# One weight transfer of a long stream, issued in three pieces of 48, 8 and 8 rows

## The chip, the cores and the metric

The kernel runs on one core of a Trainium2 chip. The metric is the device time of one execution in microseconds (us); lower is better. The core's compute engines are TensorE (PE in the profile; its weight loads are shown apart as PEld), VectorE (DVE), ScalarE (ACT) and GpSimd (POOL). SyncE (SP) and POOL issue the DMA transfers of this kernel, and 16 DMA engines carry them out.

## The reference

Linear attention with the feature map elu + 1, then a spectral mixing of its output along the sequence: a real Fourier transform, a complex matrix for each of the 64 lowest frequencies ("modes"), the inverse transform, and a channel product with a rectifier.

```python
def _attn_ref(q, k, v):                        # 8 x 8 heads x 576 x 64
    def phi(x):
        return np.where(x > 0, x, np.exp(x) - 1.0) + 1.0
    q_p, k_p = (phi(q), phi(k))
    kv = np.einsum('bhsd,bhse->bhde', k_p, v)
    z = np.sum(k_p, axis=2)
    num = np.einsum('bhsd,bhde->bhse', q_p, kv)
    den = np.einsum('bhsd,bhd->bhs', q_p, z)[..., None] + 1e-06
    return (num / den).astype(np.float32)

def _moe_ref(x, w_r, w_i, w_ch):               # w_r, w_i: 64 x 512 x 512, float32
    B, S, D = x.shape                          # 8, 576, 512
    n_modes = w_r.shape[0]
    X = np.fft.rfft(x, axis=1)
    Y = np.zeros_like(X)
    Xr, Xi = (np.real(X[:, :n_modes]), np.imag(X[:, :n_modes]))
    Yr = np.einsum('bmd,mde->bme', Xr, w_r) - np.einsum('bmd,mde->bme', Xi, w_i)
    Yi = np.einsum('bmd,mde->bme', Xr, w_i) + np.einsum('bmd,mde->bme', Xi, w_r)
    Y[:, :n_modes] = Yr + 1j * Yi
    y = np.fft.irfft(Y, n=S, axis=1)
    u = x + y
    return (u + np.maximum(u @ w_ch, 0.0)).astype(np.float32)
```

The two weight tensors `w_r` and `w_i` are read once each and are by far the largest inputs: 64 modes x 2 parts x 1 MB.

## The kernel before

**First part (lines 370 to 405).** For each of the eight batch elements q, k and v are loaded by POOL, which casts them to 16 bits on the way, the attention is formed, and its output is transformed to the 64 modes, kept as `xt_c` in SBUF. Between these loads POOL already issues the first weights.

**The weight stream.** The 64 modes are worked on as 32 pairs, `p` = 0 to 31. `mode_pair(p)` (line 462) multiplies the 16 activation slices of a pair with its weight tile `w{p}` in 16 products (line 432, PSUM tile `P`), brings the result to SBUF (`evacuate`, lines 447 and 449, DVE for even pairs and ACT for odd ones), picks the two modes out of it (line 455), and fills the time up with other work from a list (`work_slot`: folding early modes into the output, channel products and so on) and with products that only keep PE busy (`keep_warm`, line 419).

**The weight tile and its two transfers.** `w{p}` has 128 partitions. `w_load(p, half, ...)` (line 112) is called for half 0 (from `w_r`) and half 1 (from `w_i`) and issues one transfer each time, line 117. The source of one transfer is two modes, 2 x 512 x 512 float32, read as 64 rows of 16 x 512 consecutive numbers (32 KB). Row r of half h goes to partition 2r + h, as bfloat16 (16 KB): 1 MB is written for each transfer, which the DMA casts on the way.

**What sets the order.** All issues are pinned to program order (`pin`). The tiles of pairs 0 and 1 and of all pairs from 5 on share two buffers (`W_KEEP = 2`, pool `wpool`); pairs 2 to 4 have buffers of their own. `mode_pair(p)` begins with `w_get(p)`, so that the transfers of pair p are issued in the order of the code before its products; they wait on POOL until the products of the pair that had the buffer, p - 2, are done. So while pair p is in transfer or in use, pair p + 1 is in transfer. POOL issues nothing else in this part of the program. A transfer's landing is told by a semaphore, which each of the 16 DMA engines steps once when its part is done; POOL's transfers take eight semaphores in turn.

**The end.** The last pair (`w_load_last`, `last_pair`, line 487) comes in eight smaller transfers, so that its last products (`y_last`, line 513) follow each small landing. After them the last modes are transformed, and the outputs are summed (lines 760 and 800) and stored by SP (lines 816 and 822).

Of the kernel before, what the change touches and what calls it, by code (L numbers as in the profile page):

```python
# [43 lines left out]
def kernel(  # L44
# [10 lines left out]
    nc = tc.nc  # L55
# [7 lines left out]
    NDW = 4 * NDC  # L63
# [42 lines left out]
    pin = tc.keep_in_program_order  # L106
    PIECES = (slice(0, 2), slice(2, 4), slice(4, 6), slice(6, 7), slice(7, 8))
    HALVES = [slice(0, 64), slice(64, 128)]

    LAST = NM // 2 - 1  # L110

    def w_load(p: int, half: int, pool, tag: str, bufs: int):
        if half == 0:
            w_in[p] = pool.tile([128, NDW, D], BF16, tag=tag, bufs=bufs, name=f"w{p}")
        two = (moe_w_r, moe_w_i)[half][2 * p : 2 * p + 2]
        pin(
            nc.gpsimd.dma_start(  # L117
                out=w_in[p][half::2], in_=two.rearrange("g (r dc) e -> (g r) dc e", dc=NDW)
            )
        )  # L120

    def w_load_last(pool, tag: str, bufs: int):
        w_in[LAST] = pool.tile([128, NDW, D], BF16, tag=tag, bufs=bufs, name=f"w{LAST}")
        for g in range(2):
            for half in range(2):
                rows_in = (moe_w_r, moe_w_i)[half][NM - 2 + g].rearrange("(p dc) e -> p dc e", dc=NDL)
                for dcs in PIECES if (g, half) == (1, 1) else (slice(0, NDL),):
                    dst = w_in[LAST][half::2, g * NDL + dcs.start : g * NDL + dcs.stop]
                    pin(nc.gpsimd.dma_start(out=dst, in_=rows_in[:, dcs, :]))
# [16 lines left out]
    def w_next():  # L146
        p, half = pending.pop(0)
        pool, tag, bufs = (wpool, "w", W_KEEP) if p < n_keep else (wpre, "wp", W_PRE)
        w_load(p, half, pool, tag, bufs)
# [258 lines left out]
    def w_get(p: int):  # L408
        if p not in w_in and p == LAST:
            w_load_last(wpool, "w", W_KEEP)  # L410
        elif p not in w_in:
            for half in range(2):
                w_load(p, half, wpool, "w", W_KEEP)
        return w_in[p]
# [14 lines left out]
    def product(P, x, n: int, w, dc: int, n_dc: int):  # L429
        c = dc % NDC * 32  # L430
        pin(
            nc.tensor.matmul(  # L432
                P[c : c + n, :], x, w[:, dc, :],
                start=(dc < NDC), stop=(dc >= n_dc - NDC), tile_position=(0, c),
                skip_group_check=True,
            )
        )

    def set_diagonal(p: int):
        for h in range(2):  # L440
            src = xt_v[HALVES[h], :, :, :, p].rearrange("p c t b -> p c (t b)")
            pin(nc.vector.tensor_copy(out=xz[p % 2][HALVES[h], :, h, :], in_=src))  # L442
# [19 lines left out]
    def mode_pair(p: int):  # L462
# [5 lines left out]
        for dc in range(NDW):  # L468
            product(P, xz[p % 2][:, dc].rearrange("p h n -> p (h n)"), 32, w, dc, NDW)
        if p + 1 < LAST:  # L470
            set_diagonal(p + 1)
# [15 lines left out]
    def last_pair():  # L487
        xl = ystage.tile([128, NDL, 2 * B], BF16, name="xl")
        for h in range(2):
            src = xt_v[:, (2 * h + 1) * NDC : (2 * h + 2) * NDC, :, :, LAST]  # L490
            pin(
# [3 lines left out]
            )  # L495
        w = w_get(LAST)
        kk = NM - 2
# [91 lines left out]
    def x_of(t: int):  # L589
        if t < B * NJJ:  # L590
            return x_main[t // NJJ][:, t % NJJ, :]
        i = t - B * NJJ
        return x_tail[i // 2][:, i % 2, :]
# [352 lines left out]
    for h, eng in enumerate((nc.sync, nc.gpsimd)):  # L946
        eng.dma_start(
            out=YZ_all[64 * h : 64 * h + 64 : NF // NL].rearrange("r b z d -> r b (z d)"),
            in_=last.rearrange("p z d -> p (z d)"),
# [15 lines left out]
    def sums_of(n: int, i: int):  # L965
# [8 lines left out]
            out=x_of(0), in0=accs[0][:, 0], scalar=0.0, in1=x_of(0), op0=ALU.max, op1=ALU.add  # L974
# [50 lines left out]
```

## Time and profile before

| what | value |
|---|---|
| median of 3 runs | 421.13 us |
| lowest, highest | 421.12, 421.89 us |
| span of the profiled execution (first to last instruction) | 419.4 us |
| mean granted clock of TensorE | 0.830 |
| PE, DVE, ACT, POOL busy, share of the span | 76%, 55%, 37%, 14% |
| read from HBM, written | 163.93 MB, 9.44 MB |
| weight transfers of 1024 KB, real and imaginary | 31 and 31 |
| their median time from issue to landing | 13.2 and 17.5 us |
| one issue on POOL (line 117), median | 544 ns |

The page divides the span into 40 slices of about 10.5 us and gives for each the busy share of an engine in tenths. The share of the DMA is that of the core's 16 DMA engines together:

```profile
PE   0369998999617875676767686988798877998993
DMA  8999999999999999999999999999999999998698
```

The chain of waits goes back from the last instruction to what released it, and so on; a line of it has the start, the length and what it was, all in us from the start of the span. A transfer in it reaches from its issue to its landing, so that time in line behind other transfers counts in. In the lists of packets, "under 512 B" counts the small ones; a transfer's completion is a packet of 4 bytes on each DMA engine. The queue "q0 software_dynamic" carries POOL's transfers, "q1 hardware_dynamic" SP's, and the queues with "instruction" the program code of the engines. A queue's share is the time that its packets took, of 16 engines over the stretch that is looked at.

### The profile page before, as it was taken

The numbers are of one execution on the slowest core, as the hardware profiler recorded it, in microseconds if no ns is written. First come the engines' busy times: TensorE is split into PE (matmuls) and PEld (weight loads), VectorE is DVE, ScalarE is ACT, GpSimd is POOL, SyncE is SP. The second block draws the span as 40 slices with busy tenths as digits, with TensorE's granted clock in tenths as the row PEclk, the third lists the DMA queues.
The fourth block names the chain that finished last, engine by engine and source line by source line (L and its number), as shares of the span: only waits on it lengthen the run. The fifth ranks groups of instructions, "written<-read, shape, count | busy, mean of one in ns | idle before, by whom it ended". The sixth has DMA issues, their size and how long they took to land.

```text
span 419.4 us, 7466 instructions
## 1 busy us (share of the span) xinstructions
PE 317.2 (76%) x3143; PEld 164.4 (39%) x3143; DVE 231.3 (55%) x509; ACT 154.2 (37%) x253; POOL 57.4 (14%) x100
## 2 busy tenths in 40 slices
PE   0369998999617875676767686988798877998993
PEld 0257776877301332222222233433343332453421
DVE  4588899785314563463645353464456443522794
ACT  4677798854201011000000233334253432330783
POOL 4222224210011211111111111111111111130000
PEclk9999999579855658665655599899899997899998
DMA  8999999999999999999999999999999999998698
GB/s 217 211 212 216 210 222 203 228 206 223 217 223 208 218 220 209 220 217 212 220 214 213 223 213 214 223 210 216 220 209 219 217 214 219 216 209 166 235 391 328
DMA packets 17073, 93.17 MB, mean 222 GB/s; under 512 B 2112, under 2 KB 3024, under 8 KB 12880
## 3 DMA queue, kind: packets, MB, share of 16 engines
q0 software_dynamic: 12496, 81.48, 93.4%
q1 hardware_dynamic: 4544, 11.22, 7.2%
q8 instruction: 24, 0.39, 0.3%
q14 instruction: 9, 0.07, 0.0%
HBM read 163.93 MB, written 9.44 MB: 413 GB/s over the span
## 4 chain that ended last, share of the span: by engine, by line
DMA 64%; PE 23%; DVE 4%; POOL 3%; ACT 3%; issue 2%; DVEq 0%; ACTq 0%; POOLq 0%
DMA w<-in_moe_w_i_dram 53%; DMA pick_sb<-row_pick 8%; PE P L432 6%; DMA k<-in_k_dram 3%; PE acc L760 3%; PE kvp L257 3%; PE acc L800 2%; POOL w L117 2%; PE z L726 1%; DVE x L293 1%; ACT ke L208 1%; PE xf L355 1%; PE zl L419 1%; PE qTp L237 1%; PE num L163 1%
## 5 line engine op out<-in xcount | busy, mean ns | idle before, releaser
L432 PE MATMUL P<-w,xz 128*32 128x512 bf16 x496 | 42.6, 475 | 37.6 <-DMA w<-in_moe_w_i_dram 35.4
L419 PE MATMUL zl<-wch,id 128*128 128x512 f16 x185 | 58.2, 466 | 0.0
L449 ACT CAST ys<-P 128x512 f16<-128x512 f32 x15 | 8.8, 586 | 132.4 <-PE P L432 132.4
L117 POOL DMA_DIRECT2D w<-in_moe_w_r_dram x31 | 17.3, 559 | 246.4 <-PE P L432 211.8
L447 DVE CAST ys<-P 128x512 f16<-128x512 f32 x17 | 11.8, 692 | 51.0 <-PE P L432 51.0
L706 PE MATMUL eps<-wch,xTw 128*128 128x512 f16 x144 | 39.3, 399 | 0.0
L432 PEld LDWEIGHTS <-xz 128*32 128x32 bf16 x496 | 12.6, 108 | 63.3 <-DMA w<-in_moe_w_i_dram 40.3
L163 PEld LDWEIGHTS <-qT 64*128 64x128 f16 (+1 forms) x640 | 22.6, 122 | 29.6 <-issue 15.6
L689 ACT CAST x16w<-x_main 128x512 f16<-128x512 f32 x32 | 19.8, 618 | 37.8 <-DVE x_main L687 37.8
L687 DVE TENSOR_TENSOR x_main<-ya,x_main 128x512 f32<-128x512 f32 x32 | 22.0, 689 | 16.5 <-PE ya L683 16.3
L257 PE MATMUL kvp<-vpad,ke 32*128 32x130 f16 x576 | 24.3, 263 | 8.9 <-ACT qT L244 6.1
L442 DVE COPY xz<-xt_c 64x256 bf16<-64x256 bf16 x62 | 23.0, 371 | 10.9 <-PE P L432 10.0
L419 PEld LDWEIGHTS <-id 128*128 128x128 f16 x185 | 18.9, 112 | 25.6 <-issue 14.3
L714 ACT CAST E<-eps 128x512 f16<-128x512 f32 (+1 forms) x40 | 21.2, 540 | 17.7 <-PE eps L706 17.7
L257 PEld LDWEIGHTS <-ke 32*128 32x128 f16 x576 | 22.3, 116 | 10.6 <-issue 8.6
L163 PE MATMUL nw<-kv_sb,qT 64*128 64x65 f16 (+1 forms) x320 | 18.2, 231 | 9.8 <-DVE x_tail L650 4.7
L237 PE MATMUL qTp<-id,qe 128*128 128x128 f16 x144 | 15.1, 289 | 10.6 <-DVE qe L221 9.5
L293 DVE TENSOR_TENSOR x<-num,rd 128x512 f16<-128x512 f32 x32 | 22.1, 692 | 1.1
L650 DVE TENSOR_TENSOR x_main<-nw,rd 128x256 f32<-128x256 f32 x32 | 11.2, 416 | 18.8 <-PE nw L163 18.8
L455 PE MATMUL yt<-pick_sb,ys 128*128 128x32 f16 (+1 forms) x128 | 8.8, 185 | 16.7 <-DMA pick_sb<-row_pick 9.4
L698 DVE COPY xTw<-xTp 128x512 f16<-128x512 f16 x36 | 15.0, 416 | 10.3 <-PE xTp L696 10.3
L208 ACT ACTIVATE qe<-q 128x1152 f16<-128x1152 f16 (+1 forms) x16 | 17.9, 1157 | 7.2 <-DMA q<-in_q_dram 7.1
(118 smaller groups left out, 507.5 us busy)
## 6 DMA issues: line engine op xcount, KB each, us to landing
w<-in_moe_w_r_dram POOLq DMA_DIRECT2D x31, 1024.0 KB, 13.2
w<-in_moe_w_i_dram POOLq DMA_DIRECT2D x31, 1024.0 KB, 17.5
out_dram<-x_main SPq DMA_DIRECT2D x12, 512.0 KB, 3.6
k<-in_k_dram POOLq DMA_DIRECT2D x8, 576.0 KB, 12.9
v<-in_v_dram POOLq DMA_DIRECT2D x8, 576.0 KB, 14.3
q<-in_q_dram POOLq DMA_DIRECT2D x7, 576.0 KB, 12.6
out_dram<-x_main SPq DMA_DIRECT2D x8, 256.0 KB, 4.0
q<-in_q_dram SPq DMA_DIRECT2D x2, 576.0 KB, 4.5
```

Of the source, the lines that this page charges most:

```text
L117: nc.gpsimd.dma_start(out=w_in[p][half::2], in_=two.rearrange("g (r dc) e -> (g r) dc e", dc=NDW))
L163: mm = nc.tensor.matmul(num[hpo][orow, c0 : c0 + 65], qT[rows, hpp, h2, cols], kv_sb[rows, hpp, h2, :])
L208: pin(nc.scalar.activation(out=ev[:, c], in_=heads(nm, b, c), func=AF.Exp))
L257: nc.tensor.matmul(kv_ps[:, h2, 0:130], phi["k", b][r0 : r0 + 32, j // NJ, j % NJ].rearrange("p o d -> p (o d)"), vp[r0 : r0 + 32, :, j, 0 ...
L293: nc.vector.tensor_tensor(out=dst.rearrange("p (o c d) -> p o c d", o=2, c=4), in0=nv[:, :, :, 0:64], in1=rden.unsqueeze(3).broadcast_to([ ...
L419: pin(nc.tensor.matmul(last_ps[0], id16, wch16[:, 0, :]))
L432: nc.tensor.matmul(P[c : c + n, :], x, w[:, dc, :], start=(dc < NDC), stop=(dc >= n_dc - NDC), tile_position=(0, c), skip_group_check=True,)
L442: pin(nc.vector.tensor_copy(out=xz[p % 2][HALVES[h], :, h, :], in_=src))
L687: pin(nc.vector.tensor_tensor(out=x, in0=acc, in1=x, op=ALU.add))
L689: pin(nc.scalar.copy(out=x16w[t], in_=x))
L706: nc.tensor.matmul(e_ps, xT[:, c, :], wch16[:, c, :], start=(c == 0), stop=(c == NDC - 1))
L714: pin(nc.scalar.copy(out=dst, in_=e_ps[:, cols]))
```

## The change

`w_load` gets a table, `ROW_CUTS`, with one entry: for pair 21, half 0, the 64 rows are issued as three transfers, rows 0 to 47, 48 to 55 and 56 to 63. Every other pair and half has the one entry (0, 64) and is issued as before. The rows, their places in the tile, the bytes, the buffer and the order against the other issues stay the same.

```diff
     LAST = NM // 2 - 1
+    ROW_CUTS = {(21, 0): ((0, 48), (48, 56), (56, 64))}
 
     def w_load(p: int, half: int, pool, tag: str, bufs: int):
         if half == 0:
             w_in[p] = pool.tile([128, NDW, D], BF16, tag=tag, bufs=bufs, name=f"w{p}")
         two = (moe_w_r, moe_w_i)[half][2 * p : 2 * p + 2]
-        pin(
-            nc.gpsimd.dma_start(
-                out=w_in[p][half::2], in_=two.rearrange("g (r dc) e -> (g r) dc e", dc=NDW)
-            )
-        )
+        rows_in = two.rearrange("g (r dc) e -> (g r) dc e", dc=NDW)
+        for lo, hi in ROW_CUTS.get((p, half), ((0, 64),)):
+            pin(
+                nc.gpsimd.dma_start(
+                    out=w_in[p][half + 2 * lo : 2 * hi : 2], in_=rows_in[lo:hi]
+                )
+            )
```

## The prediction

> **What bounds the kernel now.** I read the chain of waits first. It names what ended last at each step, and most of the span is one kind of link:
>
> ```profile
> DMA 64%; PE 23%; DVE 4%; POOL 3%; ACT 3%; issue 2%; DVEq 0%; ACTq 0%; POOLq 0%
> DMA w<-in_moe_w_i_dram 53%; DMA pick_sb<-row_pick 8%; PE P L432 6%; DMA k<-in_k_dram 3%; PE acc L760 3%; PE kvp L257 3%; PE acc L800 2%; POOL w L117 2%; PE z L726 1%; DVE x L293 1%; ACT ke L208 1%; PE xf L355 1%; PE zl L419 1%; PE qTp L237 1%; PE num L163 1%
> ```
>
> Then the same chain in order of time around the changed transfer. The two issues at 272.58 and 273.12 are the real and the imaginary half of pair 21 (pair 5 is issued at 115.62, and one pair follows per two issues).
>
> ```profile
> 271.22 1.07 PE P L432 x16
> 272.29 0.29 issue
> 272.58 0.54 POOL w L117
> 273.12 17.50 DMA w<-in_moe_w_i_dram
> 290.62 0.04 issue
> 290.67 1.08 PE P L432 x16
> ```
>
> The reader is to see a loop: pair 19's products free a buffer, POOL issues pair 21, it lands 17.5 us later, its products free the buffer for pair 23. Two such loops interleave, so a pair takes 19.4 / 2 = 9.7 us and one transfer 4.85 us. Of the 17.5 us most is standing in line: while pair 21 is issued, pair 20 still has until about 290.62 - 9.71 = 280.9. So the chain's POOL and PE links are not what costs. The third view, the DMA queues over a stretch of the stream, says what does:
>
> ```profile
> DMA packets 662, 8.63 MB, mean 216 GB/s; under 512 B 135, under 2 KB 135, under 8 KB 135
> ...
> q0 software_dynamic: 660, 8.60, 101.2%
> q8 instruction: 2, 0.03, 0.3%
> ```
>
> That is 230 to 270 us. All 16 DMA engines are busy all the time. The 135 small packets are the 4-byte completions, 16 per transfer, so 8.4 transfers; the other 525 of q0 are 62 per transfer, which is one packet for each of the 64 rows. One row costs one engine 1.012 x 16 x 40 us / 525 = 1.23 us; the packet records start 1.21 us apart, and I use that. Four rows per engine make the 4.85 us. An engine works through its own line of rows without a gap, so the stream ends when the engine with the most work ends.
>
> Therefore the fourth view, the stages at the stream's end (columns: stage, its length, busy time of PE, PEld, DVE, ACT, POOL, clock, DMA share, GB/s):
>
> ```profile
> 380.00:384.00 4.00, 4.00 (x27) 1.57 (x28) 0.25 (x2) 0.00 (x0) 0.00 (x0) 1.00 1.00 201
> 384.00:385.00 1.00, 1.00 (x5) 0.18 (x4) 0.69 (x1) 0.00 (x0) 0.00 (x0) 1.00 0.69 127
> 385.00:386.00 1.00, 0.90 (x8) 0.28 (x7) 0.62 (x1) 0.00 (x0) 0.00 (x0) 1.00 0.64 118
> 386.00:387.00 1.00, 0.67 (x17) 0.57 (x17) 0.00 (x0) 0.00 (x0) 0.00 (x0) 1.00 0.55 95
> 387.00:388.00 1.00, 1.00 (x19) 0.60 (x17) 0.00 (x0) 0.00 (x0) 0.00 (x0) 1.00 0.24 37
> ```
>
> The DMA share falls in steps: 0.55 is 9 of 16 engines. The sixteen steps of the last weight landing in the semaphore's records say it exactly. Seven engines are done between 384.54 and 385.02, one at 386.72, one at 386.88, and seven between 387.65 and 387.88. What makes nine late is the code loading of the page's third part:
>
> ```profile
> q0 software_dynamic: 12496, 81.48, 93.4%
> q1 hardware_dynamic: 4544, 11.22, 7.2%
> q8 instruction: 24, 0.39, 0.3%
> q14 instruction: 9, 0.07, 0.0%
> ```
>
> The 24 packets of q8 are 16 KB and take 0.89 to 1.12 us each. Their durations repeat with a period of eight, and after each one single landing step falls back by about 1.1 us: eight engines take them in turn. By 386 us seven of these have had three, the eighth two (386.88). The engine at 386.72 has had only shorter q14 packets (0.32 us each). The other seven have had almost none.
>
> **The change, part by part.** Products, order, bytes and buffers stay. Removed: one POOL issue of 64 rows. Added: three issues of 48, 8 and 8 rows into the same buffer, ahead of the imaginary half.
>
> Issue: two more at 0.54 us (the row of L117), 1.09 us on POOL. Behind them stands only the imaginary half of pair 21, issued at 274.2 in place of 273.1; POOL's next work, pair 22 at 282.34, waits for products. The earliest engine needs pair 21's first row at about 280.9 - 3.34 = 277.6 and its imaginary rows 4.85 us later. All pieces are issued by then: 0. Without that line of work ahead it would be 1.09 us.
>
> Waits: pair 21's first product waits for four landings in place of two. At POOL's 0.043 us for such a wait instruction that is 0.09 us for PE, put on the step 290.62 to 292.03. Pair 22 keeps the engines busy to about 300: 0. The eight semaphores that POOL's transfers take in turn are reached two issues earlier; the transfers eight back (pairs 17 to 20) have landed when their turn comes: 0.
>
> Completions: two more transfers put two more 4-byte packets, 0.022 us each, on every engine: 0.04 us, on the path.
>
> Rows: this decides. 48 rows are three for each engine in place of four. Each 8-row piece can occupy at most eight engines, since a row is one packet. The trace of before has no transfer of fewer than 16 rows, so where the pieces go must be bounded:
> - Different eights: each engine has 3 + 1 = 4 rows as before, 0.
> - The same eight twice: these have 5 rows, +1.21 us, the others 3, -1.21 us. Only seven engines are early, so any eight hold a late one. Best case, the seven and the one at 386.72: it ends at 386.72 + 1.25 = 387.97 against 387.88 now, +0.09. With the one at 386.88: +0.25. With any of the other seven: +1.02 to +1.25.
>
> So the same eight cannot gain. I take +1.25, since nearly every choice of eight holds one of the seven latest, and keep 0 and +0.09 as the other bound. The last landing passes to the end one to one: y_last's products follow each landing within 0.05 us in the chain, and nothing behind them waits for another DMA of the stream.
>
> The Trainium skill bears on this choice, and speaks against mine. "DMA: Bandwidth & Descriptors", section "Why a DMA increments its semaphore by 16 and not by 1", says that POOL's transfers of 8 rows take eight consecutive engines from a cursor that moves round; by that the two pieces complement each other and the time would be 421.2. The same section measured an exception for some direct copies, dealt in equal shares from the first engine on; by that both pieces fall on the same eight. No run shown here tells which holds.
>
> Sum against the profiled execution: 419.4 + 1.21 + 0.04 = 420.65 us of span. The median of the runs, 421.13, is 1.73 above the span of the profiled one; with it 422.4.
>
> If an early engine runs dry, that costs nothing. After the change it can be 3.34 + 2.42 = 5.8 us ahead of the latest; pair 23's issue comes about 1.4 us after a landing, and an early engine has 9.7 - 5.8 = 3.9 us of rows left then. The late ones never run dry.
>
> **The rivals.**
> - No change, 421.2: the two pieces go to different eights, or to the eight without q8 packets (+0.04 to +0.09). For it: the pieces are issued one after the other, and a dealing that moves on evens them out. Against it: the two are alike in shape, and a dealing by shape alone repeats itself.
> - Faster, 420.0: the pieces' rows miss all nine late engines. Then the late ones lose a row, 387.88 - 1.21 + 0.04 = 386.71, and the whole ends 1.17 us earlier. It decides from the point where the engine at 386.72, too, gets none of the 16 rows, so that seven or fewer take them. For it: 1.6 us are to be had, since the mean of the sixteen ends is 386.3. Against it: one row per engine and eight rows need eight engines.
> - Much slower, 426 to 430: a piece of 8 rows stays on one engine. With one piece it has 11 rows in place of 4, +8.5 us; an early engine ends at 385 + 8.5 = 393.5, 5.6 later than now, and a late one 8.5 later. Against it: every transfer in the trace is spread.
>
> **How the numbers follow.** Forecast, same eight with a late one among them: 0.44, 422.4, with its own range 422.1 to 422.7. No change: 0.37. Faster: 0.12. Much slower: 0.07. The range 420.8 to 422.8 holds the first two with the 0.77 us by which the three runs of before differ, 0.81 in all; the faster and the much slower case are left out. About 0.2%, 0.84 us, can be told from no change: faster 0.12, same 0.37, slower 0.44 + 0.07 = 0.51.
>
> **What would show it.** Right: in the stages at the end, the DMA share keeps its long tail and the last weight landing is at about 389.1; the steps of pair 21's landing spread to 5.8 us from 3.3. No change: the spread stays at 3.3 and the stages' shares are as now. Faster: the spread shrinks to about 2.2. In all cases POOL's issues should show two more of 0.54 us, and pair 22's issue should keep its place near 282.3. I am wrong if pieces of 8 rows take another time per row than 1.21 us, or if the engines that load code are others in the next execution.

## The result, and the profile after

The changed kernel takes 422.52 us (median of 10 runs, 422.18 to 422.86), the kernel before 421.29 us beside it (10 runs, 421.12 to 421.89): a ratio of 1.0025, with a 95% interval of 1.0017 to 1.0034. So it is slower by 1.2 us, 0.25%. The forecast was 422.4.

The first view of the changed kernel's page is the count of DMA packets (the upper line is that of before) and the chain of waits by engine:

```profile
DMA packets 17073, 93.17 MB, mean 222 GB/s; under 512 B 2112, under 2 KB 3024, under 8 KB 12880
DMA packets 17121, 93.17 MB, mean 222 GB/s; under 512 B 2160, under 2 KB 3072, under 8 KB 12928
...
DMA 65%; PE 20%; DVE 6%; POOL 3%; issue 3%; ACT 2%; DVEq 0%; POOLq 0%
```

The kernel is still bound by the same chain, and as many bytes are moved. There are 48 packets more, all of them under 512 B. That is more than the 32 completions of two more transfers; the other 16 are taken up below. The next view is the chain in order of time around pair 21 (the change moves line 117 to 120 and line 432 to 435; columns are start, length, what):

```profile
272.27 0.28 issue
272.56 1.53 POOL w L120 x3
274.09 17.70 DMA w<-in_moe_w_i_dram
291.79 0.14 issue
291.93 1.07 PE P L435 x16
...
293.29 0.54 POOL w L120
```

The three pieces are issued one after the other, and the imaginary half follows at 274.09, 0.97 us later than before. It lands at 291.79, against 290.62 before: all of the loss, 1.17 us, is there at once. What the issues cost is hidden, as POOL's own order shows (columns: start, busy time, line, transfer, count, idle time before and what ended it):

```profile
272.56 1.54 POOL L120 DMA_DIRECT2D w<-in_moe_w_r_dram  x3 [7.95 <-PE P L435]
274.09 0.57 POOL L120 DMA_DIRECT2D w<-in_moe_w_i_dram  x1
282.64 0.55 POOL L120 DMA_DIRECT2D w<-in_moe_w_r_dram  x1 [7.98 <-PE P L435]
```

POOL is idle for 8 us before and after, and pair 22 is issued at 282.64 (282.34 before). Then the end of the stream, in the same stages as before (stage, length, busy time of PE, PEld, DVE, ACT, POOL, clock, DMA share, GB/s); the first line is the last stage of before, the others are those of the changed kernel:

```profile
388.00:389.00 1.00, 0.91 (x12) 0.59 (x13) 0.28 (x2) 0.17 (x1) 0.00 (x0) 1.00 0.00 0
385.00:386.00 1.00, 1.00 (x8) 0.22 (x4) 0.69 (x1) 0.00 (x0) 0.00 (x0) 1.00 0.87 154
386.00:387.00 1.00, 0.98 (x8) 0.31 (x7) 0.62 (x1) 0.00 (x0) 0.00 (x0) 1.00 0.48 80
387.00:388.00 1.00, 0.54 (x16) 0.47 (x17) 0.00 (x0) 0.00 (x0) 0.00 (x0) 1.00 0.17 31
388.00:389.00 1.00, 0.97 (x21) 0.62 (x17) 0.00 (x0) 0.00 (x0) 0.00 (x0) 1.00 0.10 16
```

Fewer engines are late, but later. At 387 to 388 us the share is 0.17, fewer than three engines, where it was 0.24; and at 388 to 389 us, where it was 0.00, two engines still work. The steps of the last weight landing in the semaphore's records agree: two engines end at 389.02 and 389.05, one at 387.84, and all others before 387.2. Before, seven ended between 387.65 and 387.88. So most of the late engines were relieved, while two were loaded further, and these two set the end. From there the difference goes through unchanged: the last landing is 1.17 us later, and the span, 420.5 us, is 1.1 us longer.

### The profile page after: what moved, and what is told of

It reads as the page before. It is cut to its first block, busy times and chain, and to the rows that moved or that the text cites. A ratio compares the mean times of both kernels' runs of the same rounds, so it can differ in the third digit from the quotient of the medians.

```text
span 420.5 us, 7470 instructions
## 1 busy us (share of the span) xinstructions
PE 326.1 (78%) x3143; PEld 168.4 (40%) x3143; DVE 231.3 (55%) x509; ACT 154.3 (37%) x253; POOL 58.3 (14%) x102
## 4 chain that ended last, share of the span: by engine, by line
DMA 65%; PE 20%; DVE 6%; POOL 3%; issue 3%; ACT 2%; DVEq 0%; POOLq 0%
DMA w<-in_moe_w_i_dram 53%; DMA pick_sb<-row_pick 8%; PE P L435 5%; DMA k<-in_k_dram 3%; PE acc L763 3%; PE kvp L260 2%; PE zl L422 2%; PE acc L803 2%; POOL w L120 2%; DVE x L296 1%; PE z L729 1%; ACT ke L211 1%; PE yb L748 1%; ACT qT L247 1%; PE xf L358 1%
## 5 line engine op out<-in xcount | busy, mean ns | idle before, releaser
L435 PE MATMUL P<-w,xz 128*32 128x512 bf16 x496 | 45.9, 507 | 33.8 <-DMA w<-in_moe_w_i_dram 31.6
L120 POOL DMA_DIRECT2D w<-in_moe_w_r_dram x33 | 18.2, 553 | 247.2 <-PE P L435 228.6
L260 PE MATMUL kvp<-vpad,ke 32*128 32x130 f16 x576 | 25.6, 272 | 8.9 <-ACT qT L247 6.1
L260 PEld LDWEIGHTS <-ke 32*128 32x128 f16 x576 | 23.4, 121 | 10.7 <-issue 8.6
L166 PE MATMUL num<-kv_sb,qT 64*128 64x65 f16 (+1 forms) x320 | 16.9, 225 | 4.4 <-DVE x L296 2.3
```

What stands on the lines that cost most here:

```text
L120: nc.gpsimd.dma_start(out=w_in[p][half + 2 * lo : 2 * hi : 2], in_=rows_in[lo:hi])
L166: mm = nc.tensor.matmul(num[hpo][orow, c0 : c0 + 65], qT[rows, hpp, h2, cols], kv_sb[rows, hpp, h2, :])
L260: nc.tensor.matmul(kv_ps[:, h2, 0:130], phi["k", b][r0 : r0 + 32, j // NJ, j % NJ].rearrange("p o d -> p (o d)"), vp[r0 : r0 + 32, :, j, 0 ...
L435: nc.tensor.matmul(P[c : c + n, :], x, w[:, dc, :], start=(dc < NDC), stop=(dc >= n_dc - NDC), tile_position=(0, c), skip_group_check=True,)
```

## The experiments

The theory (A): a transfer of fewer rows than there are DMA engines always goes to the same engines, as many as it has rows. The two pieces give the same eight engines two rows each, where an even dealing would give all sixteen one row; the late engines among the eight carry the surplus to the end. Rivals: more transfers cost time in themselves (B); the dealing moves on from transfer to transfer (C); the loss is partly given back later (D); the place in the tile or the order decides (E). Each time is compared with the kernel before in the same series, whose medians were 421.6 to 421.7 us there.

**More transfers, dealt evenly.**

```diff
-    ROW_CUTS = {(21, 0): ((0, 48), (48, 56), (56, 64))}
+    ROW_CUTS = {(21, 0): ((0, 16), (16, 32), (32, 48), (48, 64))}
```

> Four transfers of 16 rows each in place of the one of 64 rows, so three transfers more than before and one more than in the change, but every one can be dealt evenly to 16 engines. If the two 8-row pieces of the change cost 1.2 us because the same eight engines get both (theory A), this is level with before: 421.3 to 421.4 us, and the landings of the pairs after it spread over 3.3 us as before. If the cost is that of more transfers, completions or waits (theory B, 1.2 us for two), it is 421.3 + 1.8 = 423.1 us.

Measured: 421.57 us beside 421.58, a ratio of 1.0002 (0.9992 to 1.0012). The end of its stream, in the same stages:

```profile
385.00:386.00 1.00, 0.98 (x8) 0.31 (x7) 0.62 (x1) 0.00 (x0) 0.00 (x0) 1.00 0.64 117
386.00:387.00 1.00, 0.51 (x14) 0.45 (x15) 0.00 (x0) 0.00 (x0) 0.00 (x0) 1.00 0.51 90
387.00:388.00 1.00, 0.97 (x22) 0.62 (x18) 0.00 (x0) 0.00 (x0) 0.00 (x0) 1.00 0.29 45
388.00:389.00 1.00, 0.91 (x15) 0.55 (x13) 0.23 (x1) 0.00 (x0) 0.00 (x0) 1.00 0.00 0
```

The shares 0.64, 0.51, 0.29 and 0.00 are close to those of before (0.64, 0.55, 0.24, 0.00), though this kernel issues one transfer more than the change. The spread of the landings was 3.8 us where 3.3 was expected, but pair 19, ahead of the pieces, already landed over 3.75 us in this execution. B falls: issues, completions and waits of three more transfers cost nothing that can be measured.

**Twice the dose: both halves of pair 21.**

```diff
-    ROW_CUTS = {(21, 0): ((0, 48), (48, 56), (56, 64))}
+    ROW_CUTS = {(21, h): ((0, 48), (48, 56), (56, 64)) for h in range(2)}
```

> Both halves of pair 21 are cut into 48, 8 and 8 rows. Theory A, the dealing of an 8-row piece always begins at the same engine: four rows more than the others on the same eight engines, each of the eight gets 6 + 4 = 10 rows in place of 8, +2.4 us, 423.7 us; the landings spread over some 8 us, if the early engines don't run dry. Theory C, the dealing moves on in some way with each piece or transfer: the second half lands on other engines, and the time is anything from 421.3 (all evened out) to 423.7; 422.5 if the two halves' eights are half the same.

Measured: 424.28 us, a ratio of 1.0063 (1.0048 to 1.0078), +2.7 us. The chain:

```profile
272.40 2.58 POOL w L120 x5
274.99 18.08 DMA w<-in_moe_w_i_dram
...
293.11 1.92 PE P L435 x16
...
295.32 0.54 POOL w L120
```

Pair 21 lands at 293.07, 2.45 us later than before: twice the price, so the second half's pieces fell on the same eight as the first's. The steps of its last landing spread over 7.2 us (expected: some 8). Pair 23 is issued at 295.32 instead of 292.03, and that is too late for the early engines. Of these 3.29 us, 0.84 come from pair 21's products, which took 1.92 us in place of 1.08; the granted clock was 0.50 then. The DMA share in the stages from 293 us shows it:

```profile
293.00:295.00 2.00, 1.89 (x17) 0.56 (x17) 0.00 (x0) 0.00 (x0) 0.00 (x0) 0.50 0.81 172
295.00:297.00 2.00, 2.00 (x12) 0.92 (x11) 0.42 (x1) 0.88 (x2) 1.08 (x2) 0.77 0.96 180
297.00:299.00 2.00, 2.00 (x19) 1.16 (x19) 1.36 (x3) 1.39 (x3) 0.00 (x0) 1.00 0.89 172
```

Less is moved (172 and 180 GB/s, against 216 in the steady stream of before): the engines that are ahead stand still until pair 23's rows come. They lose their lead, and the time stays near +2.4. The last weight landing of this execution is at 390.91, 3.0 us after that of before, so some 0.6 us came behind pair 21; the runs do not show from where.

**Pieces of four rows.**

```diff
-    ROW_CUTS = {(21, 0): ((0, 48), (48, 56), (56, 64))}
+    ROW_CUTS = {(21, 0): ((0, 48), (48, 52), (52, 56), (56, 60), (60, 64))}
```

> 48 rows and four pieces of 4 rows. Theory A: the four pieces go to the same four engines, which have 3 + 4 = 7 rows in place of 4, +3.6 us; with a late one among them 421.3 + 3.6 = 424.9 us. If all four are early ones (they end 2.9 to 3.3 us before the latest), they end only 0.3 to 0.8 us behind the latest of before: 421.6 to 422.1 us. Theory C, the dealing moves on by the size of the piece: 16 rows on 16 engines, 421.3 us.

Measured: 424.16 us, a ratio of 1.0058 (1.0043 to 1.0073), +2.6 us. A dealing that moves on by the size of the piece is out (421.3). But neither of theory A's two values was met. 2.6 is three rows, 3.6 us, less 1.0 us; in the profile of before the latest engine but the seven ends 1.0 us before the last one (386.88 and 387.88). So the four engines would hold one of the two in the middle and none of the seven latest. That is argued from the number; the last run below tests it.

**The third piece after the imaginary half.**

```diff
-    ROW_CUTS = {(21, 0): ((0, 48), (48, 56), (56, 64))}
+    ROW_CUTS = {(21, 0): ((0, 48), (48, 56)), (21, 1): ((0, 64), (56, 64, 0))}
...
-        two = (moe_w_r, moe_w_i)[half][2 * p : 2 * p + 2]
-        rows_in = two.rearrange("g (r dc) e -> (g r) dc e", dc=NDW)
-        for lo, hi in ROW_CUTS.get((p, half), ((0, 64),)):
+        for lo, hi, *of in ROW_CUTS.get((p, half), ((0, 64),)):
+            h = of[0] if of else half
+            two = (moe_w_r, moe_w_i)[h][2 * p : 2 * p + 2]
+            rows_in = two.rearrange("g (r dc) e -> (g r) dc e", dc=NDW)
...
-                    out=w_in[p][half + 2 * lo : 2 * hi : 2], in_=rows_in[lo:hi]
+                    out=w_in[p][h + 2 * lo : 2 * hi : 2], in_=rows_in[lo:hi]
```

> The third piece of the change, 8 rows of the real half, is issued after the imaginary half's 64 rows in place of before it; sizes and number of transfers are those of the change. Theory A: the same eight again, 422.5 us, as the change. Theory C, a dealing that moves with every transfer: the two pieces fall on different eights, 421.3 us.

Measured: 422.49 us, a ratio of 1.0022 (1.0013 to 1.0032): as the change. A transfer between the pieces alters nothing. In this execution pair 21 is complete at 290.62, as before; the surplus shows at the last weight landing only, 388.88 against 387.88.

**Half the dose.**

```diff
-    ROW_CUTS = {(21, 0): ((0, 48), (48, 56), (56, 64))}
+    ROW_CUTS = {(21, 0): ((0, 48), (48, 64, 0, 8), (48, 56, 8, 16), (56, 64, 8, 16))}
...
-        for lo, hi in ROW_CUTS.get((p, half), ((0, 64),)):
+        for lo, hi, *c in ROW_CUTS.get((p, half), ((0, 64),)):
+            cols = slice(*(c or (0, NDW)))
...
-                    out=w_in[p][half + 2 * lo : 2 * hi : 2], in_=rows_in[lo:hi]
+                    out=w_in[p][half + 2 * lo : 2 * hi : 2, cols], in_=rows_in[lo:hi, cols]
```

> Of the last 16 rows of pair 21's real half, the first half of the columns goes as one transfer of 16 rows, dealt evenly; the second half of the columns goes as two pieces of 8 rows. Theory A, the same eight engines get both pieces: they have 3 + 0.5 + 1 = 4.5 rows' worth, the others 3.5, so half the price of the change, +0.6 us over before of the same job, and a spread of the landings of 3.3 + 1.2 = 4.5 us. Theory B, each small transfer or each dealing to eight engines has a price of its own whatever its length: +1.2 us or more, as in the change, since there is one transfer more than in it.

Measured: 422.01 us beside 421.62, a ratio of 1.0011 (1.0002 to 1.0020), +0.4 us and no more than 0.84: half the price fits, the whole does not. The spread was missed: pair 21's steps spread over 3.1 us, not 4.5. In this execution the two engines that were latest at that time were not among the eight; the last weight landing still came at 388.60, 0.7 us after that of before.

**Another pair.**

```diff
-    ROW_CUTS = {(21, 0): ((0, 48), (48, 56), (56, 64))}
+    ROW_CUTS = {(9, 0): ((0, 48), (48, 56), (56, 64))}
```

> The same three pieces in pair 9, some 117 us earlier in the stream. Theory A: the rows that an engine has too many stay in its line to the end, +1.2 us over before of the same job, as in the change. Theory D, the line has slack that gives time back, or the delay is taken up by a wait that is there anyway: less than the change, down to 0, since 117 us more are left for it; it would also be less if the place beside other work matters.

Measured: 423.16 us, a ratio of 1.0034 (1.0022 to 1.0047), +1.5 us with an interval of 0.9 to 2.0. Nothing is given back in 117 us more, so D falls. Whether it is more than in the change is not settled; the intervals overlap.

**The pieces first, and other rows.**

```diff
-    ROW_CUTS = {(21, 0): ((0, 48), (48, 56), (56, 64))}
+    ROW_CUTS = {(21, 0): ((0, 8), (8, 16), (16, 64))}
```

> The two 8-row pieces are rows 0 to 7 and 8 to 15, issued ahead of the 48 others: other rows of the source, other partitions of the tile, and another place in the order. Theory A, the number of rows alone sets which engines a piece goes to, always the same eight: +1.2 us over before of the same job. Theory E, the place in the tile or what was issued just before decides the engines: another value; 0 if the two pieces then fall on different eights.

Measured: 422.70 us, a ratio of 1.0026 (1.0017 to 1.0035), +1.1 us. E falls: neither the partitions nor the order change the price beyond the interval (0.7 to 1.5 us).

The dealing can also be read from the trace's packet records themselves. On one engine a row's packet begins 18 to 20 ns before the end of the row ahead of it, so the packets can be strung into sixteen lines, one for each engine. With the third piece apart (278 to 290 us) and with the pieces first (275 to 292 us), eight lines have one row of each of the two pieces, and the other eight have none of either; the changed kernel shows the same, but for two of the eight lines, which cross. With the pieces of four rows, four lines have a row of all four pieces and twelve have none.

**A try for a gain: a quarter of the columns in pieces of four rows** (with the loop of the half dose).

```diff
-    ROW_CUTS = {(21, 0): ((0, 48), (48, 56), (56, 64))}
+    ROW_CUTS = {(21, 0): ((0, 48), (48, 64, 0, 12)) + tuple((r, r + 4, 12, 16) for r in range(48, 64, 4))}
```

> A try for a gain. Of the last 16 rows of pair 21's real half, three quarters of the columns go as one even transfer of 16 rows, the last quarter as four pieces of 4 rows. With the pieces of 4 always on the same four engines (theory A), these have 3 + 0.75 + 1 = 4.75 rows' worth, +0.91 us, the twelve others 3.75, -0.30 us. The run with four whole pieces of 4 rows cost 2.6 us instead of 3.6, so the latest of the four engines ends about 1.0 us before the latest of all: then the four end at -1.0 + 0.91 = -0.1 us and the others at -0.3 us, so level with before or up to 0.1 us faster, less 0.1 us for five more transfers: 0 within what can be measured. If one of the seven latest engines were among the four, it would be +0.9 us. If small pieces had a price of their own, more than 1.2 us.

Measured: 421.25 us beside 421.74, a ratio of 0.9992 (0.9983 to 1.0001). The 0.9 us that one of the seven latest would have cost are excluded, so the four engines hold none of them in effect; five transfers more cost nothing again. Whether it is faster can't be told. In its profile the last weight landing is at 387.72 us, 0.16 before that of before, about what was expected; but the even run's came 0.18 after it, so that this is within what two executions differ by.

## Why the prediction was right

**What bounds.** The prediction took the line of rows of the most laden engine for what sets the end, and one row for 1.21 us. Half a row, one row and two rows too many gave 0.4, 1.2 and 2.7 us. The two rows cost somewhat more than twice 1.21; that remainder of 0.3 us is within the interval (2.0 to 3.3). The last weight landing was forecast at about 389.1 and came at 389.05.

**The rows.** "The same eight twice", +1.25 with a late engine among the eight, was the term that decided, and the forecast gave it 0.44 only. Between the same eight and different eights the prediction had an argument but no row that decides, so there was luck in the choice; the size that follows from it was worked out. The choice is now shown twice: by elimination (even dealing costs nothing, a transfer between the pieces, their order and their rows change nothing, and the price goes with the rows), and by the lines of packets, where the same engines have all pieces. The Trainium skill, "DMA: Bandwidth & Descriptors", section "Why a DMA increments its semaphore by 16 and not by 1", has both answers. The case agrees with its exception of equal shares from the first engine on in that the pieces always fall on the same engines; which of the sixteen these are no run shows. The section's cursor that moves round, which spoke against the forecast, would have given 421.3 for the change and for the pieces of four rows, which took 422.5 and 424.2.

**No gain possible with eight.** The argument was that only seven of the sixteen engines are early, so that any eight hold a late one. The landing steps after the change bear it out: most late engines ended 0.7 us or more before the old end, and two ended 1.17 us after it. One of the prediction's signs of being wrong did occur: the code loads began at another place in the execution after (see the end). The forecast did not need them to stay, since by this argument any eight hold a late engine.

**Issue, waits, completions.** The imaginary half was issued at 274.09 (predicted 274.2), pair 22 at 282.64 (near 282.3), and pair 21's products began 0.14 us after the landing instead of 0.04 (0.09 more were predicted). The even run shows that all this is hidden. The completions on the path, 0.04 us, are too small to be seen.

**Engines that run dry.** It was predicted that an early engine would be up to 5.8 us ahead (the steps of pair 21 spread over 5.6) and have rows left. Later in the stream that was not so: pair 30 was issued at 362.99, 3.3 us after pair 28 had landed (1.4 were taken), and its first row began at 364.53, 1.54 us after the issue, which the sum did not have. The earliest engine had finished pair 29 at 364.08, and its next landing step came after 5.87 us instead of 4.85. So it lost 1.0 us: it stood still for 0.7 us, and its first row took 1.46 us in place of 1.23. The consequence was predicted rightly: this costs nothing as the late ones go on.

**What was wrong.** Two 4-byte packets were predicted for each engine, 32 in all, and 48 came. A few rows beside the small packets took up to 1.54 us in place of 1.23, which the sum did not have. Both are inside the 0.1 us by which 1.17 at the last landing misses 1.25. The spread alone is no sure sign of the price, as the half dose showed: the sign is the time of the last step at the end.

## What to carry to other kernels

Where a DMA stream keeps all engines busy, time is set by the engine with the most work, so a transfer should have a number of rows that deals evenly; cutting one into more pieces is free as long as each piece does (three more cost nothing here, with POOL idle for 8 us around its issues), and dear as soon as the short pieces pile up on the same few engines. A surplus is not worked off later: one row too many in the full stream, at pair 9 as at pair 21, was one row at its end. Before rows are moved between engines, count in the landing steps how many engines are early: a piece that reaches more engines than that cannot help. That a piece for fewer engines does help was not shown: the one try gained nothing that can be told.

## What the runs showed of the hardware that was not expected

An engine that gets no row of a small transfer seems to send a placeholder of 4 bytes besides its completion. The packets under 512 B, 2112 before, grow by 16 for each transfer more and by 1 for each engine that a piece leaves out:

| kernel | transfers more | completions | engines left out | sum | counted |
|---|---|---|---|---|---|
| the change | 2 | 32 | 2 x 8 | 48 | 48 |
| 16 rows four times | 3 | 48 | 0 | 48 | 48 |
| both halves | 4 | 64 | 4 x 8 | 96 | 96 |
| pieces of four rows | 4 | 64 | 4 x 12 | 112 | 112 |
| half the dose | 3 | 48 | 2 x 8 | 64 | 64 |
| a quarter in fours | 5 | 80 | 4 x 12 | 128 | 128 |

The count fits in these six kernels, and in the three others with two 8-row pieces (48 each); what the packet is for is not shown.

The code loads of queue q8 take the eight engines in turn, but do not always begin at the same one. The first two q8 packets took 936 and 974 ns in the profile of before, 974 and 962 after, 948 and 945 with the third piece apart: always the same ring of eight durations, entered at another place. The ten profiles show four such places, and in the order of the record each kernel of a series begins two places after the one ahead of it. So which engines have had three loads when the stream ends, and which are the latest, differs between the profiles. That is not the cause of the loss: pair 19, ahead of the pieces, lands at 271.00 to 271.37 us in all nine profiles without pieces in pair 9, wherever their code loads begin. Whether the place also changes between executions of one kernel, and has a part in the 0.3 to 1.9 us by which these differ, was not tried.
